# Reordering the vector and GpSimd queues around two block boundaries of a fused attention and GEGLU kernel

## The chip, the cores and the metric

The kernel runs on one core of a Trainium2 chip. The metric is the device time of one execution in microseconds (us). All runs quoted were correct. A run of a program on one core is called fast or slow by comparison with the fastest run of the same kernel. Engines are abbreviated as in the profile: PE is TensorE's matmul, PEld its weight load, DVE is VectorE, ACT is ScalarE, POOL is GpSimd, and SP is the queue that issues transposes and stores. Tiles that PE writes lie in PSUM, in pieces called banks that are used again and again; the other tiles lie in SBUF. Most blocks of tokens reach PE through a DMA transpose, written `xT<-t` in the profile.

## The reference, cut to what matters

Eight batches of 576 tokens go through a linear attention with a norm over each head, and the 4608 resulting rows of 512 go through a gated feed-forward layer with a gated residual.

```python
kv  = einsum('bhsd,bhse->bhde', k, v)
out = einsum('bhsd,bhde->bhse', q, kv)
x   = out / sqrt(mean(out*out, -1) + 1e-6) * g_norm      # 4608 x 512 in all
hid = gelu(x @ w_gate) * (x @ w_val)                     # 512 -> 1536
y   = x + sigmoid(x @ w_res) * (hid @ w_out)             # 1536 -> 512
```

## The kernel before

The rows are worked in nine blocks of 512. While PE multiplies block m, the other engines prepare the attention of a later batch. Large products are done as seven products of sums instead of eight plain ones (A, D, E, F below are PSUM accumulators), so DVE also has to form sums of weights, of tokens (`ts`) and of hidden rows (`hid_s`). In block 2 the first four slices of the hidden layer are plain products (gps and vps), and eight more come as two groups of seven products.

The end of a block, with DVE's gates (`pf`), POOL's additions of x (`fin`), and places (`aside`) at which other work is queued:

```python
def others():
    prod(w["A"], s_[1], wo_t[:, 1], False)
    aside("F")                                   # the norm of a later batch, on POOL
    sub(nc.vector, w["F"], w["A"], w["d"], ALU.add)
    aside("00")                                  # token sum 0 of the next block, on DVE
    prod(w["E"], a_of(blk, 1, 2), b_of(2, 1), False)
    pf((0, 0), w["E"])
    aside("22")                                  # token sum 1
    prod(w["A"], s_[2], wo_t[:, 2], False)
    c22 = res_all[part((1, 1))]
    sub(nc.vector, c22, w["A"], w["d"], ALU.add)
    aside("01")                                  # token sum 2
    prod(w["F"], s_[3], b_of(2, 2), False)
    pf((0, 1), w["F"])
    if not later:                                # later is true in block 1 alone
        fin((0, 0))
    aside("11")                                  # token sum 3
    prod(w["A"], a_of(blk, 2, 2), wo_t[:, 3], False)
    pf((1, 1), c22)
    pf((1, 0), w["A"])
    if later:
        return
    fin((0, 1)); store(0); fin((1, 1)); fin((1, 0)); store(1)      # shortened
```

Block 1 leaves its multiplies of x by g (`a_x`, on DVE) and its additions to block 2's two groups of products (0 and 1), where they are queued behind named steps:

```python
if later:
    x = [lambda j=j: a_x(blk, j) for j in range(NJ)]
    at_word(blk + 1, 0, "h21", *x[0:2], lambda: fin((0, 0)), lambda: fin((0, 1)), lambda: store(0))
    at_word(blk + 1, 1, "Fv", x[2])
    at_word(blk + 1, 1, "h21", x[3], lambda: fin((1, 0)), lambda: fin((1, 1)), lambda: store(1))
```

Behind the second group POOL issues the loads of a later batch, and behind those stands the norm (`a_norm`, fifteen small operations, L300 to L312). The norm's result scales rows on DVE (`a_t`), and these scalings stand in DVE's queue ahead of the next block's first hidden product.

Of the kernel before, what the change touches and what calls it, by code (L numbers as in the profile page):

```python
# [18 lines left out]
def kernel(  # L19
# [17 lines left out]
    B, H, S, D = q.shape  # L37
# [3 lines left out]
    NF = F // P  # L41
# [302 lines left out]
    def a_x(b, j, eng=nc.vector):  # L344
        blk, jj = where(b, j)
        eng.tensor_tensor(out=t_t[blk][:, jj, :], in0=t_t[blk][:, jj, :], in1=g16, op=ALU.mult)
# [56 lines left out]
    def m_res(blk, j, bank):  # L403
        rps = pmoe.tile([P, C], FP32, name="rps", bank=bank)
        for cc in range(NP):
            nc.tensor.matmul(  # L406
                rps,
                lhsT=xT_t[blk][:, j, cc, :],
                rhs=wr16[:, cc, :],
                start=(cc == 0),  # L410
                stop=(cc == NP - 1),
            )

        th = th_all[:, j, :]
        nc.scalar.activation(out=th, in_=rps, func=AF.Tanh, scale=0.5)  # L415
        return th

    def m_sigmoid(j):
        th = th_all[:, j, :]
        nc.scalar.activation(out=th, in_=th, func=AF.Copy, scale=0.5, bias=0.5)  # L420
# [26 lines left out]
    def b_of(i, j):  # L447
        return wo16[:, (i - 1) * NFH : i * NFH, (j - 1) * CH : j * CH]

    def a_of(blk, i, j):  # L450
        return hids[blk][:, (j - 1) * NFH : j * NFH, (i - 1) * PR : i * PR]

    def sub(eng, out_, in0, in1, op=ALU.subtract):
        eng.tensor_tensor(out=out_, in0=in0, in1=in1, op=op)
# [17 lines left out]
    def s_last(blk):  # L472
        sub(nc.vector, hid_sums[3], a_of(blk, 1, 2), hid_sums[1])

    def prod(ps, a, b, start, es=(0, 1)):

        for e in es:
            for f in range(NFH):
                nc.tensor.matmul(  # L479
                    ps[:, e - es[0], :],  # L480
                    lhsT=a[:, f, e * P : (e + 1) * P],
                    rhs=b[:, f, :],
                    start=(start and e == es[0] and f == 0),
                    stop=(f == NFH - 1),
                    skip_group_check=True,
                )

    def out_by_products(blk, later, banks, amid):
        w = {}
        s_ = hid_sums  # L490

        def aside(ahead_of):
            for f in amid.get(ahead_of, ()):
                f()

        def res(jj):
            for j in (2 * jj, 2 * jj + 1):
                m_res(blk, j, banks[j])

        def first_two():  # L500
            for n in ("D", "E", "F", "A"):
                w[n] = pmoe.tile([P, 2, CH], FP32, name="w" + n, bank=banks[n])
            w["d"] = finp.tile([P, 2, CH], FP32, tag="wd", bufs=1, name="wd")
            s_last(blk)
            prod(w["A"], a_of(blk, 1, 1), b_of(1, 1), True)
            nc.scalar.copy(out=w["E"], in_=w["A"])
            aside("D")
            prod(w["D"], s_[0], wo_t[:, 0], True)
            nc.scalar.copy(out=w["d"], in_=w["D"])
            aside("gates")  # L510
            for j in range(NJ):
                m_sigmoid(j)

        def part(jj):
            return slice(None), slice(2 * jj[0], 2 * jj[0] + 2), slice(jj[1] * CH, (jj[1] + 1) * CH)

        def pf(jj, src):
            nc.vector.tensor_tensor(out=res_all[part(jj)], in0=th_all[part(jj)], in1=src, op=ALU.mult)  # L518

        def fin(jj):  # L520
            of = part(jj)
            nc.gpsimd.tensor_tensor(out=res_all[of], in0=res_all[of], in1=t_t[blk][of], op=ALU.add)  # L522

        def store(jj):
            dst = out[blk * S : blk * S + M0, :].rearrange("(p j) c -> p j c", j=NJ)
            js = slice(2 * jj, 2 * jj + 2)
            nc.sync.dma_start(out=dst[:, js, :], in_=res_all[:, js, :])

        def others():


            prod(w["A"], s_[1], wo_t[:, 1], False)
            aside("F")
            sub(nc.vector, w["F"], w["A"], w["d"], ALU.add)
            aside("00")
            prod(w["E"], a_of(blk, 1, 2), b_of(2, 1), False)
            pf((0, 0), w["E"])
            aside("22")
# [3 lines that stand above are left out]
            aside("01")  # L542
            prod(w["F"], s_[3], b_of(2, 2), False)
            pf((0, 1), w["F"])
            if not later:
                fin((0, 0))
            aside("11")
            prod(w["A"], a_of(blk, 2, 2), wo_t[:, 3], False)
            pf((1, 1), c22)
            pf((1, 0), w["A"])  # L550
            if later:

                return
            fin((0, 1))
            store(0)
            fin((1, 1))
            fin((1, 0))
            store(1)

        if later:  # L560
            x = [lambda j=j: a_x(blk, j) for j in range(NJ)]
            at_word(blk + 1, 0, "h21", *x[0:2], lambda: fin((0, 0)), lambda: fin((0, 1)), lambda: store(0))
            at_word(blk + 1, 1, "Fv", x[2])
            at_word(blk + 1, 1, "h21", x[3], lambda: fin((1, 0)), lambda: fin((1, 1)), lambda: store(1))
        return [lambda: res(0), lambda: res(1), first_two, others]

    def out_last(blk, banks):
# [66 lines left out]
    LAST = (B - 1, B)  # L634
    GF = 4
# [43 lines left out]
    def token_sums(blk, eng):  # L679
        def one(i, x, y):  # L680
            if i == 0:
                x_sums[blk] = stage.tile([P, 4, 2, 2, P], FP16, tag="ts", name="ts")
            t = x_sums[blk]
            x_, y_ = (t[:, n] if isinstance(n, int) else x_quadrant(blk, *n) for n in (x, y))
            sub(eng, t[:, i], x_, y_)

        return [
            lambda: one(0, (0, 1), (0, 0)),
            lambda: one(1, (1, 1), 0),
            lambda: one(2, (1, 1), (0, 1)),  # L690
            lambda: one(3, (1, 0), 1),
        ]
# [114 lines left out]
    for which in "kv":  # L807
        if which == "k":
            t = hidp.tile([P, NF, NJ * P], FP16, tag="hid", name=which + "f").rearrange("p a b -> p (a b)")
        else:  # L810
            t = hid_s
# [8 lines left out]
    for which in "kv":  # L820
        t = hid_of[which]
# [308 lines left out]
    def at(blk, slot, *fs):  # L1130
        plans[blk].setdefault(slot, []).extend(fs)

    def aside_out(blk, ahead_of, *fs):
        amid_out.setdefault(blk, {}).setdefault(ahead_of, []).extend(fs)
# [19 lines left out]
    GROUPS = {blk: (1, 2) for blk in range(2, B - 1)} | {B - 1: (1, 0, 2), B: (0, 1, 2)}  # L1154
    amid_gv = {}

    def at_word(blk, i, word, *fs):
        amid_gv.setdefault((blk, i), {}).setdefault(word, []).extend(fs)
# [48 lines left out]
    at(B - 2, NF + 1, *late_sums[4:8])  # L1207
    for blk in GROUPS:
        t = token_sums(blk, nc.vector)
        for key, f in zip(("00", "22", "01", "11"), t):  # L1210
            aside_out(blk - 1, key, f)
    out_at = {}

# [34 lines left out]
    for blk in range(B + 1):  # L1248
# [21 lines left out]
        else:  # L1270
# [32 lines left out]
            def products(blk=blk, outs=outs):  # L1303
                s_rest(blk)
                if blk not in GROUPS:
                    out_at[blk] = banks_behind()
                if blk < B:
                    outs.extend(out_by_products(blk, blk == 1, out_at[blk], amid_out.get(blk, {})))
                else:
                    outs.extend(out_last(blk, out_at[blk]))  # L1310
# [54 lines left out]
```

## Time and profile before

| | before |
|---|---|
| time, the first three runs | 330.12 us median (329.43 to 330.67) |
| span of the profiled execution | 328.4 us |
| PE busy in it | 317.6 us |
| PE's waits behind the opening that can be removed | 1.65 us at 91.36; 1.65, 0.24 and 0.09 us at 132.17, 137.18 and 139.01 |

The prediction below shows the lines for these. One more line of the page belongs here: the shares, by engine, of the chain of work that ended last.

```profile
PE 82%; DVE 6%; POOL 5%; DMA 3%; issue 2%; ACT 0%; DVEq 0%; POOLq 0%; ACTq 0%
```

The chain is PE's own work for 82% of the span. The rest is two detours, one through a DMA transpose and DVE, the other through POOL and DVE. They are longer than PE's waits, because the chain runs through other engines while PE still works on something else; how long PE itself waits must be read on PE.

### The profile page before, as it was taken

What the parts mean: (1) busy time and instruction counts of PE and PEld (TensorE: products, weight loads), DVE (VectorE), ACT (ScalarE), POOL (GpSimd) and SP (SyncE); (2) the same over time, 40 slices, a digit from 0 to 9 for tenths busy, and PEclk for the clock granted to TensorE, in tenths of its full rate; (3) what the DMA queues carried; (4) which work ended last, traced back from release to release, by engine and by line L of the source; (5) the groups of instructions that cost most, each with busy time, mean ns of one, the idle gap of its engine ahead of it and who ended that gap; (6) DMA issues with size and microseconds to landing.
All of it is one profiled execution on the core that took longest, in us unless ns stands there. A gap on an engine that the chain in (4) does not pass through costs nothing.

```text
span 328.4 us, 7217 instructions
## 1 busy us (share of the span) xinstructions
PE 317.6 (97%) x2840; PEld 227.1 (69%) x2840; DVE 261.3 (80%) x474; ACT 193.3 (59%) x351; POOL 143.5 (44%) x222
## 2 busy tenths in 40 slices
PE   8999999999989999899999999999999999999993
PEld 3545655445848785686768686868587888788882
DVE  5777879679598995988887888697889877687754
ACT  3764676465537782668376846674465466636660
POOL 2783333574701498428731974115511331051232
PEclk9999999999999999999999999999999999999998
DMA  8999999898985349577949693800340030011004
GB/s 251 322 204 204 195 204 161 181 189 122 180 85 109 100 98 187 157 140 92 135 147 143 73 153 130 162 1 3 128 82 0 8 123 1 2 64 66 0 3 128
DMA packets 76692, 38.87 MB, mean 118 GB/s; under 512 B 42098, under 2 KB 74354, under 8 KB 76658
## 3 DMA queue, kind: packets, MB, share of 16 engines
q0 software_dynamic: 38752, 17.17, 41.7%
q1 hardware_dynamic: 37328, 20.71, 24.4%
q10 hardware_dynamic: 578, 0.52, 0.5%
q8 instruction: 22, 0.36, 0.5%
q14 instruction: 12, 0.10, 0.1%
HBM read 38.80 MB, written 9.44 MB: 147 GB/s over the span
## 4 chain that ended last, share of the span: by engine, by line
PE 82%; DVE 6%; POOL 5%; DMA 3%; issue 2%; ACT 0%; DVEq 0%; POOLq 0%; ACTq 0%
PE Av L723 9%; PE Ag L723 9%; PE gps L386 9%; PE wA L479 8%; PE vps L386 8%; PE rps L406 7%; PE Fv L723 4%; PE Fg L723 4%; PE fps L423 3%; DMA xT<-t 3%; PE w L479 2%; PE Eg L723 2%; PE Ev L723 2%; PE idle L888 2%; PE wF L479 2%
## 5 line engine op out<-in xcount | busy, mean ns | idle before, releaser
L760 POOL TENSOR_TENSOR hid<-ge,c 128x512 f16<-128x512 f16 x17 | 19.8, 1164 | 88.2 <-ACT ge L754 88.2
L723 PEld LDWEIGHTS <-ws 128*128 128x128 f16 x544 | 53.0, 98 | 7.0 <-issue 0.4
L374 ACT ACTIVATE ge<-gps 128x512 f16<-128x512 f32 x40 | 23.7, 597 | 53.5 <-PE gps L386 53.4
L522 POOL TENSOR_TENSOR osb<-osb,t 128x512 f32<-128x512 f32 x28 | 33.5, 1221 | 25.1 <-DVE osb L518 21.9
L479 PEld LDWEIGHTS <-hid_s 128*128 128x128 f16 x384 | 37.6, 98 | 4.3
L386 PE MATMUL vps<-xT,wv 128*128 128x512 f16 x152 | 39.0, 379 | 1.5 <-DVE hid L375 1.5
L386 PE MATMUL gps<-xT,wg 128*128 128x512 f16 x152 | 39.0, 379 | 0.0
L375 DVE TENSOR_TENSOR hid<-ge,vps 128x512 f16<-128x512 f16 x40 | 27.2, 683 | 9.8 <-PE vps L386 8.8
L406 PE MATMUL rps<-wr,xT 128*128 128x512 f16 x144 | 33.4, 380 | 0.0
L479 PEld LDWEIGHTS <-hid 128*128 128x128 f16 x288 | 28.2, 98 | 6.7 <-issue 1.7
L386 PEld LDWEIGHTS <-wv 128*128 128x128 f16 x152 | 14.9, 98 | 19.6 <-issue 1.8
L386 PEld LDWEIGHTS <-wg 128*128 128x128 f16 x152 | 14.7, 98 | 16.4 <-issue 0.2
L415 ACT ACTIVATE th<-rps 128x512 f32<-128x512 f32 x36 | 21.1, 595 | 8.1 <-PE rps L406 8.1
L744 DVE TENSOR_TENSOR Fg<-Ag,d 128x512 f32<-128x512 f32 x17 | 11.9, 700 | 15.7 <-PE Ag L723 11.6
L254 DVE TENSOR_REDUCE ss<-sq 128x8 f32<-128x512 f32 x32 | 20.1, 677 | 4.7 <-ACT sq L249 4.7
L406 PEld LDWEIGHTS <-xT 128*128 128x128 f16 x144 | 13.5, 98 | 14.2
L723 PEld LDWEIGHTS <-wg 128*128 128x128 f16 x204 | 19.7, 98 | 3.7
L723 PEld LDWEIGHTS <-wv 128*128 128x128 f16 x204 | 20.0, 98 | 2.3
L754 ACT ACTIVATE ge<-c 128x512 f16<-128x512 f32 x17 | 10.7, 630 | 17.1 <-DVE c L744 17.1
L479 PE MATMUL wA<-wo_ts,hid_s 128*128 128x256 f16 x168 | 20.6, 273 | 0.0
L332 DVE TENSOR_TENSOR t<-op,ny 128x512 f16<-128x512 f32 x28 | 18.3, 683 | 2.9 <-POOL ny L312 2.8
L723 PE MATMUL Av<-ts,ws 128*128 128x256 f16 x136 | 20.4, 272 | 0.1
(185 smaller groups left out, 716.7 us busy)
## 6 DMA issues: line engine op xcount, KB each, us to landing
out_dram<-osb SPq DMA_DIRECT2D x14, 512.0 KB, 2.6
qraw<-in_q_dram POOLq DMA_DIRECT2D x7, 512.0 KB, 7.1
k<-in_k_dram POOLq DMA_DIRECT2D x7, 512.0 KB, 9.6
v<-in_v_dram POOLq DMA_DIRECT2D x7, 512.0 KB, 11.7
wg<-in_moe_w_gate_dram POOLq DMA_DIRECT2D x2, 512.0 KB, 8.4
wv<-in_moe_w_val_dram POOLq DMA_DIRECT2D x2, 512.0 KB, 8.9
wo<-in_moe_w_out_dram POOLq DMA_DIRECT2D x2, 512.0 KB, 13.6
out_dram<-osb SPq DMA_DIRECT2D x4, 256.0 KB, 4.4
```

The costliest lines, as they stand in the source:

```text
L254: nc.vector.tensor_reduce(out=out_, in_=sqs.pop((b, i)), op=ALU.add, axis=mybir.AxisListType.X)
L332: nc.vector.tensor_tensor(out=t, in0=o, in1=scale, op=ALU.mult)
L374: nc.scalar.activation(out=ge, in_=gps, func=AF.Gelu)
L375: nc.vector.tensor_tensor(out=hids[blk][:, f, :], in0=ge, in1=vps, op=ALU.mult)
L386: nc.tensor.matmul(ps[:, j0 * P : j1 * P], lhsT=w[:, cc, :], rhs=xT_t[blk][:, j0:j1, cc, :], start=(cc == 0 and j0 == 0), stop=(cc == NP - ...
L406: nc.tensor.matmul(rps, lhsT=xT_t[blk][:, j, cc, :], rhs=wr16[:, cc, :], start=(cc == 0), stop=(cc == NP - 1),)
L415: nc.scalar.activation(out=th, in_=rps, func=AF.Tanh, scale=0.5)
L479: nc.tensor.matmul(ps[:, e - es[0], :], lhsT=a[:, f, e * P : (e + 1) * P], rhs=b[:, f, :], start=(start and e == es[0] and f == 0), stop=( ...
L522: nc.gpsimd.tensor_tensor(out=res_all[of], in0=res_all[of], in1=t_t[blk][of], op=ALU.add)
L723: nc.tensor.matmul(out_[:, r, :], lhsT=lhsT, rhs=rhs, start=(first and r == 0 and c == 0), stop=(c == 1), skip_group_check=True,)
L744: nc.vector.tensor_tensor(out=dst, in0=ps["A", u], in1=sb["d", u], op=ALU.add)
L760: eng.tensor_tensor(out=dst, in0=ge[q], in1=source(q, "v"), op=ALU.mult)
```

## The change

Its intent is to take both detours out: DVE shall not stand before a late transfer while PE needs its gates, and POOL shall have block 1's additions behind it earlier. The diff is reordering only.

```diff
             pf((0, 1), w["F"])
-            if not later:
-                fin((0, 0))
             aside("11")
             prod(w["A"], a_of(blk, 2, 2), wo_t[:, 3], False)
-            pf((1, 1), c22)
-            pf((1, 0), w["A"])
+            if len(GROUPS.get(blk + 1, ())) * GF < NF or blk + 1 >= LAST[0]:
+                pf((1, 1), c22)
+                pf((1, 0), w["A"])
+            else:                       # never reached with this kernel's groups
+                pf((1, 0), w["A"])
+                pf((1, 1), c22)
+            aside("end")
             if later:
                 return
-            fin((0, 1))
-            store(0)
-            fin((1, 1))
-            fin((1, 0))
-            store(1)
+            for i in (1, 0):
+                fin((i, i))
+                fin((i, 1 - i))
+                store(i)
 ...
-            at_word(blk + 1, 0, "h21", *x[0:2], lambda: fin((0, 0)), lambda: fin((0, 1)), lambda: store(0))
-            at_word(blk + 1, 1, "Fv", x[2])
-            at_word(blk + 1, 1, "h21", x[3], lambda: fin((1, 0)), lambda: fin((1, 1)), lambda: store(1))
+            at_word(blk + 1, 0, "Fv", x[0])
+            at_word(blk + 1, 0, "h21", *x[1:3], lambda: fin((0, 0)), lambda: fin((0, 1)), lambda: store(0))
+            at_word(blk + 1, 1, "Fv", x[3], lambda: fin((1, 0)), lambda: fin((1, 1)), lambda: store(1))
 ...
         t = token_sums(blk, nc.vector)
-        for key, f in zip(("00", "22", "01", "11"), t):
+        if blk == 2:
+            at(blk - 1, NF + 3, *t)
+            continue
+        whole = blk == B - 2 and len(GROUPS[blk]) * GF == NF      # never true
+        for key, f in zip(("00", "22", "01", "end" if whole else "11"), t):
             aside_out(blk - 1, key, f)
```

Part 1 is the last hunk (token sums of block 2), part 2 the middle one (block 1's rows in block 2), part 3 the first (POOL's additions in blocks 2 to 7).

## The prediction

> **What bounds the kernel now.** I read the page's busy shares first, then TensorE's (PE's) waits, then the timelines of PE, VectorE (DVE) and GpSimd (POOL) around each wait.
>
> ```profile
> PE 317.6 (97%) x2840; PEld 227.1 (69%) x2840; DVE 261.3 (80%) x474; ACT 193.3 (59%) x351; POOL 143.5 (44%) x222
> ```
>
> PE is busy 317.6 of 328.4 us. No part of the change removes a matmul, so it can win only PE's gaps. The waits of PE, longest first:
>
> ```profile
> PE wA L479 <- DVE osb L454: 1.5, 1, 1.5
> PE vps L386 <- DVE hid L375: 1.5, 1, 1.5
> ```
>
> Everything else in that list is at most 0.3 us or lies in the opening, which the change doesn't touch. The PE timeline places the two (start, duration, idle before in brackets):
>
> ```profile
> 88.40 1.47 PE L479 MATMUL wF<-wo,hid_s 128*128 128x256 f16 x12
> 91.36 1.47 PE L479 MATMUL wA<-wo_ts,hid 128*128 128x256 f16 x12 [1.49 <-DVE osb L454]
> ...
> 129.66 1.03 PE L386 MATMUL gps<-xT,wg 128*128 128x512 f16 x4
> 132.17 1.02 PE L386 MATMUL vps<-xT,wv 128*128 128x512 f16 x4 [1.48 <-DVE hid L375]
> ...
> 136.50 0.60 PE L723 MATMUL Ag<-ts,ws 128*128 128x256 f16 x4
> 137.18 0.60 PE L723 MATMUL Av<-ts,ws 128*128 128x256 f16 x4
> ```
>
> A product of 12 normally starts 1.31 us after the one before, four 512-column matmuls 0.86 us, four 256-column ones 0.44 us (the starts of neighbours that don't wait). So the losses, start to start, are 91.36-88.40-1.31 = 1.65 us at the end of block 1, 132.17-129.66-0.86 = 1.65 us early in block 3, and behind it 137.18-136.50-0.44 = 0.24 us; one more of 0.09 us at 139.01 is worked out alike.
>
> Cause of the first, on the DVE timeline:
>
> ```profile
> 86.05 0.70 DVE L454 TENSOR_TENSOR wF<-wA,wd 128x512 f32<-128x512 f32 x1 [0.25 <-PE wA L479]
> 89.15 0.51 DVE L454 TENSOR_TENSOR ts<-xT 128x512 f16<-128x512 f16 x1 [2.40 <-DMA xT<-t]
> 89.69 0.69 DVE L518 TENSOR_TENSOR osb<-th,wE 128x512 f32<-128x512 f32 x1
> 90.29 0.42 DVE L454 TENSOR_TENSOR ts<-xT,ts 128x512 f16<-128x512 f16 x1
> 90.63 0.68 DVE L454 TENSOR_TENSOR osb<-wA,wd 128x512 f32<-128x512 f32 x1
> ```
>
> The first token sum (ts) of block 2 stands in DVE's queue ahead of block 1's gates and waits 2.40 us for the transpose that brings block 2's tokens: the chain of waits shows that transfer as 9.72 us from 79.40, so landing at 89.12. The sum osb<-wA,wd, the last reader of wA before its last product, then runs at 90.63 rather than when its operands were ready, and PE waits for it.
>
> Cause of the second, on the POOL timeline, with the same stage one block later below it:
>
> ```profile
> 114.58 3.64 POOL L522 TENSOR_TENSOR osb<-osb,t 128x512 f32<-128x512 f32 x2 [1.85 <-DVE t L346]
> 118.91 0.98 POOL L120 DMA_DIRECT2D qraw<-in_q_dram  x1 [0.32 <-issue]
> 124.46 0.49 POOL L300 TENSOR_SCALAR nm<-ss 128x40 f32<-128x40 f32 x1
> 129.93 0.27 POOL L312 TENSOR_TENSOR ny<-na,ny 128x40 f32<-128x40 f32 x1
> ...
> 156.59 0.22 POOL L300 TENSOR_SCALAR nm<-ss 128x40 f32<-128x40 f32 x1 [1.68 <-DVE ss L254]
> 162.55 0.27 POOL L312 TENSOR_TENSOR ny<-na,ny 128x40 f32<-128x40 f32 x1
> ```
>
> In block 2, POOL adds x to the last two quarters of block 1 (3.64 us), then issues the next batch's loads, and only then starts the norm chain, at 124.46. That is 1.75 us before block 3's first matmul (126.21). In block 3 it starts at 156.59, 5.13 us before block 4's first (161.72), having waited only for the sums of squares, and no PE wait follows. DVE idles 2.81 us at 130.23 for the late norm; the hidden product queued behind that scaling frees the bank that the 132.17 matmul writes.
>
> **What the Trainium skill says.** "PSUM — Partial Sum Buffer", section "Engine vs sequencer instructions", says the queues of ScalarE, VectorE and GpSimd are strict FIFO. The trace agrees: the gates at 89.69 needed nothing of the transpose, yet stood behind the 2.40 us. "SBUF — State Buffer", section "Who interferes with whom", says a DVE instruction with two SBUF inputs contends with a GpSimd instruction that reads SBUF, and that one with at most one SBUF input, outside the 2-port modes, doesn't. The trace agrees: POOL's additions usually take about 1.15 us but 3.64 for two beside DVE's sums of hid, one of which took 1.80 instead of 0.95 us; the gate with both inputs in SBUF took 1.64 us at 260.64, beside an addition, and 0.76 elsewhere.
>
> **The change, part by part.** It adds and removes no instruction; it reorders queues. (Two new conditions for blocks with only grouped products are never met: only block 6 would qualify by its number, and it has two groups, not three.)
>
> Part 1, block 2's four token sums go behind block 1's gates. The gates then run at their operands' pace: in block 3 the sum on wA starts 1.52 us after its product (159.30 against 157.78), so here at 87.09+1.52 = 88.61, done 89.30, before the last product can start at 88.40+1.31 = 89.71. The 1.65 us go. The first user of block 2's tokens then starts at 89.71+1.31 = 91.02, still 1.9 us behind the landing. What it costs: DVE ends the last gate at about 91.9, runs four sums at 0.34 us each (the pace of two queued additions of that shape, 0.75 us) to 93.2, two scalings at 0.60 to 94.4, and the first hidden product of block 2 to 95.1. PE needs that bank at 91.02+5x0.864 = 95.34. It fits by 0.2 us.
>
> Part 2, block 1's tail in block 2. One multiply of x goes behind the first group's sums, where DVE idles 0.38 us before 103.71 and the multiply's pace is 0.34. The last two POOL additions move up into the second group, behind a multiply that ran at 109.35. By the old clock they run at about 110.2 to 112.5, beside DVE work with a PSUM input. POOL's hidden product follows, ending near 113.6 (up to 114.7 if DVE's sum takes the port first) instead of 112.73; its reader comes at about 115. The loads start near 115 instead of 118.91 and take 5.5 us; the norm then waits for the sums of squares, which end at 121.0. It starts at 121.1 to 121.8, takes about 6.2 us as in block 3, and ends near 127.3 to 128 instead of 130.2. The scalings must start by 128.6: PE needs the bank at 126.21+5x0.864 = 130.53, two scalings and a product take 1.9. So the 1.65, 0.24 and 0.09 us go.
>
> Part 3, POOL's additions behind the last gates. In blocks 2 to 5 the norm already holds them until then; only their order changes. In blocks 6 and 7 they start after 261.4 instead of at 257.91, four by 1.15 end at 266.0, and the next POOL product starts at 266.44. The slowed gate of 1.64 us falls to about 0.76, but no PE wait follows it today: worth 0.0 us.
>
> Sum: 1.65+1.65+0.24+0.09 = 3.63 us, less an estimated 0.1 us for the tight spot of part 1. From 140 us to the last matmul no PE wait listed exceeds 0.3 us, so PE work that begins earlier ends earlier, and the tail is unchanged. 330.12-3.63+0.1 = 326.6 us, 1.1% less.
>
> **The rivals.** (a) DVE takes the wait over: the sums now stand ahead of block 2's first hidden product, and the margin is 0.2 us. For it: that product has already slipped 0.3 us today. Against: DVE has idle gaps from then to 102 us. It would give back 0.2 to 0.6 us: 326.8 to 327.2. (b) The norm stays late: POOL's hidden product or the loads are held by the port or a buffer. For it: 0.6 to 1.3 us of margin rests on an estimated queue. Against: blocks 3 and 4 run this same order without a wait. If all of it stayed: 328.5. (c) The transpose holds PE itself at the first matmul of block 2. It would have to land over 1.9 us later than in this trace; the change starts nothing before it. Each us beyond is 1 us back. (d) In blocks 6 and 7 POOL's later additions delay its hidden product. The margin is 0.4 us, and the readers come 4 us or more later: nothing lost.
>
> **Range and chances.** Both causes removed, with noise of the runs (329.43 to 330.67), makes 325.9 to 327.2; I stretch the top to 327.8 for (a) and part of (b). 2% would need 323.5, 3 us beyond all removable gaps; slower by 2% would need a new wait of 10 us where I found margins of at most a few.
>
> **What would show it.** Right: no PE wait on osb<-wA,wd or hid over 0.3 us; ts behind the fifth gate with no wait on the transpose; the norm in block 2 starting some 5 us before block 3's first matmul, preceded by a wait for ss; a gate th,osb of 0.76 us in blocks 6 and 7; PE's busy time still near 317.6. Wrong: a PE wait near 95 us on a hidden product, the 2.81 us idle of DVE for ny still there, or PE waiting for xT at 91.

## The result, and the profile after

The changed kernel took 327.14 us in the median of four runs (326.66 to 327.33), the kernel before beside it 329.77 us (four runs, 329.38 to 330.67). The ratio is 0.9914 with a 95% interval of 0.9889 to 0.9940. A ratio here is the mean time of one kernel's fast runs over that of the other's of the same rounds, so it is not quite the ratio of the medians. The gain of 0.6 to 1.1% is clear of zero. All outputs are right. The profiled execution, at 326.66 us, was the fastest of the four.

The page after, its busy shares and the shares of its last chain:

```profile
span 324.9 us, 7212 instructions
...
PE 317.1 (98%) x2840; PEld 227.1 (70%) x2840; DVE 259.2 (80%) x474; ACT 193.1 (59%) x351; POOL 142.7 (44%) x222
...
PE 96%; DVE 3%; issue 0%; DVEq 0%
```

PE has the same number of matmuls and almost the same busy time in a span 3.5 us shorter, and both detours have left the chain: POOL and DMA no longer appear in it. The list of PE's waits after, whole (engine, line, what it waited for, us in total, times, longest):

```profile
PE idle L889 <- DVE zeros L860: 1.2, 1, 1.2
PE vps L1013 <- DVE t L987: 0.3, 1, 0.3
PE gps L1013 <- ACT xT L1004: 0.2, 1, 0.2
PE vps L1013 <- POOL wv L1042: 0.2, 1, 0.2
PE xtp L997 <- DVE t L987: 0.2, 1, 0.2
```

All five lie in the opening. The two of 1.5 us are gone. The PE timeline after, at the two places:

```profile
89.70 1.47 PE L479 MATMUL wA<-wo_ts,hid 128*128 128x256 f16 x12
91.01 1.03 PE L386 MATMUL gps<-xT,wg 128*128 128x512 f16 x4
...
128.01 1.03 PE L386 MATMUL gps<-xT,wg 128*128 128x512 f16 x4
128.87 1.03 PE L386 MATMUL vps<-xT,wv 128*128 128x512 f16 x4
```

The last product of block 1 starts at 89.70 instead of 91.36, and the third vps of block 3 follows its gps by 0.86 us instead of 2.51. Stage by stage, starts read from the two PE timelines:

| start of | before | after | ahead by |
|---|---|---|---|
| block 2's first gps | 92.67 | 91.01 | 1.66 |
| block 3's first gps | 126.21 | 124.56 | 1.65 |
| block 3's first grouped product (Ag) | 134.75 | 131.46 | 3.29 |
| block 3's first output product (wA) | 152.54 | 148.93 | 3.61 |
| the last product | 321.45 | 317.91 | 3.54 |
| end of the span | 328.4 | 324.9 | 3.5 |

The gain is made in two steps at the two places that the prediction names, and the 170 us behind give back 0.07 us, the size of one new small wait at 275.18 us. The DVE timeline after shows part 1:

```profile
88.60 0.69 DVE L454 TENSOR_TENSOR osb<-wA,wd 128x512 f32<-128x512 f32 x1 [0.57 <-PE wA L479]
...
91.22 0.69 DVE L518 TENSOR_TENSOR osb<-th,wA 128x512 f32<-128x512 f32 x1
91.82 0.42 DVE L454 TENSOR_TENSOR ts<-xT 128x512 f16<-128x512 f16 x1
...
94.49 0.67 DVE L375 TENSOR_TENSOR hid<-ge,vps 128x512 f16<-128x512 f16 x1
```

The sum osb<-wA,wd now waits for PE's product, where before PE waited for it. The token sums come behind the last gate, when the transpose has landed. The first hidden product of block 2 ends at 95.16; PE writes its bank at 95.33. The POOL timeline after shows part 2:

```profile
108.37 2.28 POOL L522 TENSOR_TENSOR osb<-osb,t 128x512 f32<-128x512 f32 x2 [0.36 <-DVE t L346]
110.61 1.16 POOL L761 TENSOR_TENSOR hid<-ge,c 128x512 f16<-128x512 f16 x1
...
113.19 0.98 POOL L120 DMA_DIRECT2D qraw<-in_q_dram  x1 [0.32 <-issue]
...
119.43 0.22 POOL L300 TENSOR_SCALAR nm<-ss 128x40 f32<-128x40 f32 x1 [0.77 <-DVE ss L254]
```

The two additions take 2.28 instead of 3.64 us and are over before the hidden product. The norm starts at 119.43, which is 5.13 us before block 3's first gps (124.56), and it waits for its own input, ss, as it did in the later blocks before the change. The scalings on DVE, which waited for it before, no longer do. First before, then after:

```profile
130.23 1.29 DVE L332 TENSOR_TENSOR t<-op,ny 128x512 f16<-128x512 f32 x2 [2.81 <-POOL ny L312]
```

```profile
125.70 1.29 DVE L332 TENSOR_TENSOR t<-op,ny 128x512 f16<-128x512 f32 x2
```

DVE and POOL still hinder each other in block 2, at another place: DVE's sum of hidden rows at 110.74 takes 1.84 us beside POOL's hidden product, where 0.95 is usual. No PE wait follows.

### The profile page after: what moved, and what is told of

It reads as the page before. It is cut to its first block, busy times and chain, and to the rows that moved or that the text cites. A ratio compares the mean times of both kernels' runs of the same rounds, so it can differ in the third digit from the quotient of the medians.

```text
span 324.9 us, 7212 instructions
## 1 busy us (share of the span) xinstructions
PE 317.1 (98%) x2840; PEld 227.1 (70%) x2840; DVE 259.2 (80%) x474; ACT 193.1 (59%) x351; POOL 142.7 (44%) x222
## 4 chain that ended last, share of the span: by engine, by line
PE 96%; DVE 3%; issue 0%; DVEq 0%
PE wA L479 11%; PE gps L386 10%; PE vps L386 10%; PE rps L406 10%; PE Ag L724 9%; PE Av L724 9%; PE Fv L724 5%; PE Fg L724 5%; PE fps L423 3%; PE wF L479 3%; PE wD L479 3%; PE wE L479 3%; PE w L479 2%; PE Ev L724 2%; PE Eg L724 2%; PE idle L889 2%
## 5 line engine op out<-in xcount | busy, mean ns | idle before, releaser
L522 POOL TENSOR_TENSOR osb<-osb,t 128x512 f32<-128x512 f32 x28 | 31.6, 1159 | 26.3 <-DVE osb L518 24.9
L724 PE MATMUL Ag<-ts,ws 128*128 128x256 f16 x136 | 20.4, 273 | 0.0
```

Source lines behind the costliest of these rows:

```text
L522: nc.gpsimd.tensor_tensor(out=res_all[of], in0=res_all[of], in1=t_t[blk][of], op=ALU.add)
L724: nc.tensor.matmul(out_[:, r, :], lhsT=lhsT, rhs=rhs, start=(first and r == 0 and c == 0), stop=(c == 1), skip_group_check=True,)
```

## The experiments

Wait sizes below are from start to start of PE's instructions, less the usual step, as in the prediction; the bracket in a line gives the idle time alone, which is about 0.16 us less.

### The whole change again, and its three parts alone

These four ran on one chip, five rounds each. The kernel before took 330.58 us beside them (eleven runs, 329.21 to 332.58).

**again**: the changed kernel, no edit.

> The changed kernel once more, for a closer size. If the two waits of TensorE that the trace of before shows (1.65 us, and 1.65+0.24+0.09 us) are the whole of it, the ratio is near 0.9893 (3.5 of 329.8 us). If some of the gain is lost in most runs and the profiled one was only a good one, it stays near 0.9914 (2.8 us).

It took 326.77 us (326.57 to 327.29), ratio 0.9884 (0.9853 to 0.9914). That is a little more than the 0.9893 that the two waits would give, and the two intervals overlap. So the 2.8 us of the first series was no lucky high; the two series can't be told apart.

**p1**: the kernel before with part 1 alone.

```diff
         t = token_sums(blk, nc.vector)
+        if blk == 2:
+            at(blk - 1, NF + 3, *t)
+            continue
```

> Before with part 1 alone: block 2's token sums behind block 1's gates. Theory (the two waits are separate): the wait wA<-osb goes, 1.65 us; the wait of the 512-column vps matmul on hid in block 3 stays at about 1.5 us, since POOL's order in block 2 is as before; ratio near 0.995. Rival (one late stage caused both waits): both go and the ratio is that of the whole change, near 0.99. Rival (DVE takes the wait over): a new wait of 0.2 us or more on the first hidden product of block 2, near 95 us.

It took 328.53 us (328.50 to 328.99), ratio 0.9939 (0.9911 to 0.9966), which holds the expected 0.995; the two traces differ by 1.7 us. Among the waits of PE one of the two is left:

```profile
PE vps L386 <- DVE hid L375: 1.5, 1, 1.5
```

It is 1.64 us from start to start, with 0.23 and 0.09 behind it, as before. The two waits have separate causes, and DVE did not take the first one over.

**p2**: the kernel before with part 2 alone (the middle hunk of the change).

> Before with part 2 alone: block 1's multiplies of x and its last two POOL additions spread over block 2's groups. Theory: the wait wA<-osb at 91 us stays (1.5 us), the one on hid near 132 us goes with the two small ones behind it: 1.98 us, ratio near 0.994; the norm chain on POOL starts about 5 us before block 3's first matmul. Rival: that wait comes from the late first one, and stays when that stays: ratio near 1.000.

It took 328.34 us (327.57 to 328.75), ratio 0.9927 (0.9897 to 0.9956). The wait on hid is gone, as expected, and so are the two small ones. But the other wait did not keep its expected 1.5 us. The PE timeline:

```profile
89.03 1.47 PE L479 MATMUL wF<-wo,hid_s 128*128 128x256 f16 x12
90.73 1.47 PE L479 MATMUL wA<-wo_ts,hid 128*128 128x256 f16 x12 [0.22 <-DVE osb L454]
```

It is 90.73-89.03-1.31 = 0.39 us in this execution, which may be why the ratio is below the expected 0.994. The reason is in the transfer: the transpose of block 2's tokens took 8.4 us here, 9.7 in the profile of before, and 9.9 in that of p3 below, and the waits were 0.39, 1.65 and 1.89 us. From the first to the second, both grow by 1.3 us; from the second to the third, both by 0.2. DVE itself waited 1.12, 2.40 and 2.62 us for it, each time 0.73 to 0.75 us more than PE. So beyond some 0.7 us the transfer's lateness is passed on to PE one for one, and the size of the wait is not a constant of the kernel.

The traces also show what goes with the transfer's time. It ran beside the loads that POOL issues at the same moment in twelve profiles (all but those of xt_first and dve4). Where POOL's first load started 0.03 to 0.26 us ahead of the transpose (nine profiles, before and p3 among them), the transpose took 8.6 to 10.3 us; where it started 0.07 to 0.18 us behind (p2, pool4, dve4b), 7.2 to 8.6 us. That the order makes the difference is likely from this, but no run changed the order by so little.

**p3**: the kernel before with part 3 alone (lines joined here).

```diff
-            if not later:
-                fin((0, 0))
 ...
-            fin((0, 1)); store(0); fin((1, 1)); fin((1, 0)); store(1)
+            for i in (1, 0):
+                fin((i, i)); fin((i, 1 - i)); store(i)
```

> Before with part 3 alone: POOL's additions behind the last gates in blocks 2 to 7. Theory: no TensorE wait depends on it; ratio 1.000 within 0.001; the gate th,osb in blocks 6 and 7 falls from 1.64 to about 0.7 us without any effect. Rival: the additions' contention with DVE costs time, then up to 2x0.9 us = 0.5% faster.

It took 330.33 us (329.06 to 330.79), ratio 0.9984 (0.9954 to 1.0015): no effect that these runs can tell from none. Both waits of PE stayed. The gate with both inputs in SBUF, in the view by tile (durations in ns, least, median, greatest), first before and then in p3:

```profile
L518 DVE TENSOR_TENSOR osb<-th,osb x7: 681/757/1645, 92.5 to 291.6; 128x512 f32<-128x512 f32 x7
```

```profile
L518 DVE TENSOR_TENSOR osb<-th,osb x7: 684/754/760, 92.8 to 291.9; 128x512 f32<-128x512 f32 x7
```

The slow instances disappear, and no time goes with them, because PE doesn't wait for DVE there.

### Without part 3

**p12**: parts 1 and 2 without part 3.

> Parts 1 and 2 without part 3 (POOL's additions of x keep their places in blocks 2 to 7). Theory (part 3 is worth nothing): as the whole change, ratio 0.988 to 0.991, no TensorE wait over 0.3 us behind the opening, the gate th,osb 1.64 us in blocks 6 and 7. Rival (part 3 is needed once the waits are gone, because with the earlier norm the additions of block 2 would start ahead of the gates): a TensorE wait in block 3, ratio 0.992 or more.

It took 327.12 us (326.55 to 327.67), ratio 0.9926 (0.9881 to 0.9972) against runs of before that spread from 328.55 to 331.24. The ratio is above what was expected and lies where the rival put it, but its interval is wide, and pool2 below, the changed kernel with additions that cost PE nothing, came to 0.9918 beside the same runs of before. The trace decides: PE's list has no wait behind the opening, and the slow gate of 1.645 us is back without harm. Parts 1 and 2 are the change; a value of part 3 below some 0.4 us, the difference of the two medians, can't be excluded by the times.

### Is the first wait the order of DVE's queue, or the transfer?

**xt_first**: the kernel before; block 1's loads on POOL are made to wait for the transpose.

```diff
-            at(m, NF, lambda: load_behind(b))
+            at(m, NF, lambda: load_behind(b, 2))     # first reads block 2's transposed tokens
```

> The kernel before, with one edit: POOL issues the loads of block 1 only when the transpose of block 2's tokens has landed. Theory (the transpose takes 8.4 to 9.9 us because three loads of 512 KB run beside it): it lands within 5 us of its issue, the first token sum doesn't wait, the wait wA<-osb goes (1.65 us in the trace of before). Its price by the same queue reasoning: the loads start about 4 us later, block 1's norm ends near 94.4 instead of 90.8, DVE's first hidden product of block 2 near 96.3, and TensorE waits 0.9 us there; the wait in block 3 stays. Net ratio near 0.998. Rival (the transpose is that slow by itself): it still takes 8 us or more and the wait of 1.65 us stays, plus the late norm: ratio 1.000 to 1.010.

It took 330.78 us (330.50 to 331.59), ratio 1.0039 (1.0001 to 1.0078), so slower where a small gain was expected. The mechanism was right: the transpose landed 4.3 us after its issue instead of 9.7, the first token sum did not wait, and the wait on osb was gone. The view by tile of this transpose says:

```profile
DMA to landing us min/median/max: 4.3/4.3/4.3
```

The price was mis-sized. The PE timeline of this run, and then POOL's:

```profile
95.16 1.03 PE L386 MATMUL gps<-xT,wg 128*128 128x512 f16 x4
97.81 0.38 PE L386 MATMUL vps<-xT,wv 128*128 128x512 f16 x1 [1.62 <-DVE hid L375]
```

```profile
85.03 0.98 POOL L120 DMA_DIRECT2D qraw<-in_q_dram  x1 [0.37 <-ACT wE L506]
...
95.59 0.25 POOL L312 TENSOR_TENSOR ny<-na,ny 128x32 f32<-128x32 f32 x1
```

The loads started at 85.03 and pushed the norm's end to 95.84, where 94.4 had been expected (0.7 us of the difference is a later opening in this execution; the loads, with that taken off, started 5.1 us later than in before, not 4). A new wait of 97.81-95.16-0.86 = 1.79 us stands where 0.9 had been expected. By the traces the exchange costs 1.79-1.65 = 0.14 us. The measured 0.4% is 1.3 us; the rest is the opening and the spread of the runs, and the interval reaches down to 1.0001. So the first wait can be removed from the side of the transfer too, but POOL's late loads then delay the norm, as in the second wait.

The Trainium skill, "DMA: Bandwidth & Descriptors", section "Issuing engines are not separate DMA queues", says that DMAs started by different engines run on the same 16 DMA engines and interleave. The traces fit that: the transpose, issued from SP's queue, took 9.7 us beside three loads of 512 KB and some smaller ones from POOL's queue, and 4.3 us ahead of them.

### What of part 2 removes the second wait?

Part 2 moves both DVE's multiplies and POOL's additions. Two kernels have part 1 and one half of part 2 each; only the lines added for part 2 are shown. Both must multiply x's last row earlier, at "Fv" of the second group. The kernel before took 329.71 us beside them (seven runs, 328.55 to 331.24).

**p1_fins**: the additions move, no row is spread into the first group.

```diff
+            at_word(blk + 1, 0, "h21", *x[0:2], lambda: fin((0, 0)), lambda: fin((0, 1)), lambda: store(0))
+            at_word(blk + 1, 1, "Fv", *x[2:4], lambda: fin((1, 0)), lambda: fin((1, 1)), lambda: store(1))
```

> Part 1, and of part 2 only the place of POOL's last two additions of block 1 (behind the second group's sums); block 2's first group keeps x rows 0 and 1, and rows 2 and 3 are both multiplied just ahead of the additions. Theory A (the additions' place on POOL is what delayed the norm): the wait of vps on hid in block 3 (1.64 us in part 1 alone) goes, norm start about 5 us before block 3's first matmul; ratio near 0.989, with perhaps 0.1 to 0.4 us lost to a TensorE wait in the second group, where DVE has one more multiply (0.34 us) ahead of the sums c. Theory B (the spreading of the rows on DVE is what matters): the 1.64 us stay, ratio near 0.994.

It took 327.34 us (326.62 to 327.69), ratio 0.9928 (0.9883 to 0.9973). The wait on hid is gone; the largest loss behind 110 us is 0.16 us, in block 5, which the kernel before has too. The loss feared in the second group did not come.

**p1_rows**: the rows are spread, the additions stay behind POOL's hidden product.

```diff
+            at_word(blk + 1, 0, "Fv", x[0])
+            at_word(blk + 1, 0, "h21", *x[1:3], lambda: fin((0, 0)), lambda: fin((0, 1)), lambda: store(0))
+            at_word(blk + 1, 1, "Fv", x[3])
+            at_word(blk + 1, 1, "h21", lambda: fin((1, 0)), lambda: fin((1, 1)), lambda: store(1))
```

> Part 1, and of part 2 only the rows: x rows spread as in the whole change, but POOL's last two additions stay behind its hidden product, at the old place. Theory A: they start when that product ends instead of 1.85 us later, take 2.3 to 3.6 us beside DVE's sums of hid, so the norm starts 2 to 3 us earlier than in part 1 alone and the wait of 1.64 us falls to between 0 and 0.4 us; ratio 0.989 to 0.991. Theory B (only the place on POOL counts): at least 1.2 us of the wait stay, ratio 0.993 or more.

It took 327.68 us (327.47 to 328.09), ratio 0.9942 (0.9906 to 0.9979). The additions, on POOL's timeline:

```profile
111.44 3.73 POOL L522 TENSOR_TENSOR osb<-osb,t 128x512 f32<-128x512 f32 x2
```

They start as soon as the hidden product ends, but take 3.73 us beside DVE's sums of hidden rows. The wait falls from 1.64 to 0.52 us, with 0.24 behind it. This wait lies a little outside what theory A said and far from theory B. The rest of theory A missed: the norm started at 122.14, some 1.3 us earlier than in p1 once that run's earlier opening is taken off, not 2 to 3, and the ratio lies where theory B put it. The earlier multiply alone is worth 1.1 of the 1.64 us, and the place ahead of the hidden product, with the additions running in 2.27 us in p1_fins, takes the rest. Spreading a row into the first group isn't needed for it, as p1_fins shows.

### How wide are the margins?

**pool2** and **pool4**: the changed kernel with useless additions on POOL between the loads and the norm of block 2.

```diff
                 at(m, 2 * GF, lambda: load_behind(b))
+            if m == 2:
+                at(m, 2 * GF, *[lambda: sub(nc.gpsimd, zeros, zeros, zeros)] * 4)     # or 2
```

> The changed kernel with two useless additions of 128x512 on POOL (2.3 us) between the loads and the norm of block 2. Theory with the margin of the trace: 0.77 us of idle and 1.3 us of slack of the first hidden product in block 3 absorb 2.1 us, so a wait of vps on hid of 0.0 to 0.4 us; ratio 0.989 to 0.990. Without such a margin: the wait would be 1.2 us or more.

> The changed kernel with four useless additions of 128x512 on POOL (about 1.15 us each, 4.6 us) between the loads and the norm of block 2. Theory (the norm's end holds DVE's scalings, these the first hidden product of block 3, this a PSUM bank): POOL had 0.77 us idle there, so the norm starts 3.8 us later, the first hidden product ends near 131.4 where TensorE wants the bank at 128.87: a wait of vps on hid of about 2.5 us comes back (0.75% slower than the whole change, ratio near 0.996), with some 0.3 us of small ones behind it. Rival (POOL's order didn't cause that wait): no wait over 0.3 us, ratio near 0.989.

With two (2.25 us) it took 326.73 us (326.63 to 327.35), ratio 0.9918 (0.9875 to 0.9962), and PE had no new wait over 0.07 us. With four it took 329.01 us (328.84 to 329.60), ratio 0.9985 (0.9948 to 1.0022): 2.28 us more than with two, so the whole second half of the gain is lost. The POOL and PE timelines with four:

```profile
119.32 4.60 POOL L454 TENSOR_TENSOR zeros<-zeros 128x512 f16<-128x512 f16 x4
124.01 0.28 POOL L300 TENSOR_SCALAR nm<-ss 128x40 f32<-128x40 f32 x1
```

```profile
131.54 1.02 PE L386 MATMUL vps<-xT,wv 128*128 128x512 f16 x4 [1.80 <-DVE hid L375]
```

The wait is 1.96 us rather than the 2.5 expected, because the norm takes 5.6 instead of 6.2 us there, probably since, late as it is, it meets less of DVE's work. The 0.23 and 0.09 us that followed the second wait before the change come back too, 2.28 us in all. So the norm's end governs that wait, and about 2 us of POOL time are free in the changed kernel.

**dve4**: the changed kernel with four useless additions on DVE behind the token sums.

```diff
-            at(blk - 1, NF + 3, *t)
+            at(blk - 1, NF + 3, *t, *[lambda: sub(nc.vector, zeros, zeros, zeros)] * 4)
```

> The changed kernel with four useless additions of 128x512 (0.34 us each in a row, 1.36 us) on DVE behind block 2's token sums. The trace of the change has the first hidden product of block 2 end at 95.16, and TensorE needs its bank at 95.33. Theory (margin of 0.17 us, rival (a) of the prediction just missed): a wait of vps on hid of 1.0 to 1.3 us near 95.3; 0.35% slower than the whole change, ratio near 0.993. If the margin were wide: no wait, ratio near 0.989.

Its profiled execution took 847.67 us, with all matmuls at little more than a third of their pace; the profile is of no use for this question. Its three other runs took 328.06 to 328.26 us, ratio 0.9955 (0.9913 to 0.9998). **dve4b** is the same kernel again:

> The same kernel as dve4 again, because dve4's profiled execution ran 847.7 us with matmuls at about a third of their pace, while its other three took 328.1 to 328.3. Theory as there: a wait of vps on hid of 1.0 to 1.3 us near 95.3 to 96 us in the trace, other waits of TensorE as in the changed kernel, time near 328.1 us; a margin that is wide would show no such wait.

It took 328.22 us (328.12 to 328.33), ratio 0.9938 (0.9869 to 1.0008). Its DVE and PE timelines:

```profile
93.27 1.80 DVE L454 TENSOR_TENSOR zeros<-zeros 128x512 f16<-128x512 f16 x4
94.99 1.28 DVE L332 TENSOR_TENSOR t<-op,ny 128x512 f16<-128x512 f32 x2
```

```profile
96.92 1.02 PE L386 MATMUL vps<-xT,wv 128*128 128x512 f16 x4 [1.44 <-DVE hid L375]
```

The four additions delay DVE by 94.99-93.27 = 1.72 us, more than the 1.36 assumed, probably since each reads what the one before wrote: in this trace the second token sum, which reads the first, starts 0.45 us after it, and the third, which reads neither, 0.34 us later. The wait is 1.60 us, so all but 0.12 us of the delay reaches PE. The margin is real and even smaller than the 0.17 us between DVE's end and PE's start, of which PE needs some (0.05 us here). Rival (a) of the prediction was missed by that much. No version that was run is faster than the changed kernel beyond the noise.

## Why the prediction was right

**The sum.** It said 3.63 us less 0.1; the two traces differ by 3.5 us, and PE's starts by 3.54 to 3.61. The median of the runs, 327.14 us, lies 0.5 us above the predicted 326.6 and inside the range of 325.9 to 327.8; the second series gave 326.77. Beside each other the medians differ by 2.63 us in the first series and 3.81 in the second. That the two traces fit the sum to a tenth is partly luck: the first term is the size of a wait in one execution, and p2 and p3 show that it could have been sampled at 0.39 or 1.89 us.

**Part 1.** The steps held to a few hundredths: osb<-wA,wd at 88.60 (said 88.61), the last product at 89.70 (89.71), the first hidden product of block 2 ending at 95.16 (95.1), with the bank wanted at 95.33 (95.34). The transfer was as late as before (9.6 us), and neither DVE nor PE waited for it. The allowance of 0.1 us for the tight spot was not used in the profiled run. p1 alone shows the part by itself.

**Part 2.** In the changed kernel's clock, which runs 1.65 us ahead of the old one there, the additions were to start near 108.5 and did at 108.37, the loads near 113.3 and did at 113.19, the norm between 119.4 and 120.1 and did at 119.43, ending at 125.66 where 125.6 to 126.3 had been said. p2 shows the part by itself, p1_fins and p1_rows that it acts through POOL's order and through when its input is ready, and pool4 that a late norm by itself brings the wait back.

**Part 3.** It was said to be worth 0.0 us, and p3 and p12 show no value. The slowed gate fell to 0.68 us in block 6 (257.03), where about 0.76 had been said.

**The rivals.** (a) was missed by 0.12 to 0.17 us, shown by dve4b. (b) did not come; p1_rows shows how it would have looked, with 0.52 us of the wait left. (c) did not come: the transpose landed 9.6 us after its issue at 79.39, near 89.0, still 2 us ahead of block 2's first gps; in the profile of p1_fins, where it took 10.3 us, 1.3 us were left. (d) did not come: POOL was free 0.5 us before its next product in block 7.

**What was off.** One term was treated as a constant: the 1.65 us of the first wait. It is the lateness of a transfer that took from 8.4 to 9.9 us in the three traces in which DVE stood before it beside the loads, and the wait went from 0.39 to 1.89 us with it. It would fit that kernels in which DVE doesn't stand before that transfer are steadier: beside each other, before spread over 3.4 us (eleven runs), p1 over 0.5 and the changed kernel over 0.7 (six each). But p2, which keeps that wait, spread over 1.2 us, hardly more than p12 and p1_fins without it (1.1). That it is this transfer in the unprofiled runs is argued, not shown. Another part of the spread is the opening, where PE's waits for DVE differ between executions (0.3 us in the profile after, 0.6 in that of the second series). By it block 1's last but one product starts at 88.3 to 88.4 us in six of the profiles, at 88.6 in one and at 89.0 to 89.1 in six, whatever the kernel; the changed kernel took 326.66 us in the one case and 327.29 in the other. So one median can lie half a microsecond off while the steps of the prediction hold.

## What to carry to other kernels

When an engine that releases another one's buffers stands in its own queue before work whose input may be late, put that work behind the releases, and work out the new queue to the tenth of a microsecond, because the next reader may have less than 0.2 us to spare. On an engine whose idle time looks ample, what matters is the order at one place: a few microseconds of deferred additions ahead of a norm were worth 2 us of the whole kernel, while moving POOL's additions in six other blocks, in two of them to a later time, had no value that could be measured. A wait caused by a transfer has a size that varies from run to run, so a single profile gives one sample of it.

## What the Trainium skill lacked or had wrong

- "DMA: Bandwidth & Descriptors" gives an effective bandwidth for transposes and says that transfers interleave, but not how much longer a transpose takes beside other loads. Here that of 512 rows of 512 took 4.3 us ahead of three loads of 512 KB and 7.2 to 10.3 us beside them (twelve profiles).
- "SBUF — State Buffer", section "Who interferes with whom", calls the port pair that DVE and POOL share an exclusive lock, and the traces fit that; it gives no number for work as interleaved as this. POOL's two additions took 2.28 us where DVE had PSUM inputs and 3.63 to 3.73 us beside DVE's sums of two SBUF inputs, and such a sum 1.80 to 1.84 instead of 0.95 us.
- "TensorE: Matmul & The Clock Gate", section "Seeing it yourself", warns that the clock gate's records can be unreliable and that the gate has been seen stuck at a quarter for over 50 us. In one execution of dve4, 512-column matmuls mostly started 0.62 us apart instead of 0.22 for the whole 846 us (0.59 in the mean, 0.37 of the pace), and DVE and ACT kept nearly their usual busy time. The run lists a granted clock of 1.00, but its page has no row PEclk, which the pages of the other runs have: the trace holds no record of the clock, so the 1.00 says nothing. One such execution came in all the runs; why is open.
